# Larger VectorE instructions in the attention, attention weights by offset in DRAM, and four pairs of h scaled when made

## Chip, cores and metric

The kernel runs on 1 core of one Trainium2 chip. The metric is the device time of one execution in microseconds. Engine names: TensorE (PE in the profile, PEld for its weight loads), VectorE (DVE), ScalarE (ACT), GpSimd (POOL), SyncE (SP, which issues DMAs).

## The reference

Sequence 2048, model width 1024, bf16. Two branches and a gate:

```
g = sigmoid((x * gate_w).sum(-1))                        # one number per position
q, k, v = x @ wqkv                                       # 32 heads of 32
logits[h, s, w] = q[h, s] . k[h, s - 2 w] / sqrt(32)     # w = 0..7, masked before the start
a = (sum over w of softmax(logits)[h, s, w] * v[h, s - 2 w]) @ wo
b = (gelu(x @ w_gate) * (x @ w_up)) @ w_down             # hidden width 3584
out = g * a + (1 - g) * b
```

The attention looks at 8 positions per query only, so its products are elementwise work for VectorE and not matmuls.

## The kernel before

The sequence is cut into two halves `s` of 1024 positions. The large products use the Strassen-Winograd scheme: 7 products of quarter size in place of 8, with sums and differences of the operands (the "forms") made by VectorE.

**Units.** The first part of the program is a list of 78 units. Each one makes two 128-row tiles of q and k, of v, or of one pair of the gate or up projection for one half: 7 products of 4 matmuls each, 28 matmuls of 128x512 (L366). A unit overlaps the next: `p1` (L376) of the unit, `p73` (L398) of the unit before, then `p5`, `p26` and `p4` (L406). In `p73` VectorE adds two banks (L403); `p4` writes to one of those banks again, so TensorE waits at `p4` until L403 is done. VectorE takes its instructions in order, so L403 stands behind whatever was put in VectorE's queue earlier.

**Background work.** Between units, `run_bg` (L442) hands out other VectorE work. Each piece is a generator that issues one instruction and yields its planned cost in microseconds; `run_bg` adds 4.7 or 4.8 to `credit` per unit (more where the unit has extra matmuls) and takes pieces by priority while the credit is over 0.3. This is decided when the program is built, so the cost values order the instructions and nothing is decided on the chip. The pieces that matter here:

- `qk_prods` (L610): q times the 8 shifted k of a block of 256 positions, one 128x2048 instruction per block (`qk_mult`, L597, at L598). Three of four blocks of each half are done from the unit's tile; the fourth is `spill` (L639), which multiplies (L598) and adds (L649). TensorE reduces the products over the head with a matrix of ones (L603).
- `softmax`, `softmax_exp` (the exponential, on ScalarE, L697), `softmax_back` (L700): the weights of a block, in `attn_all` as 32 partitions for each quarter `j` of 64 positions. L712 stores them on GpSimd's queue to `w_d`, one DMA for each `j`.
- `pv_all` (L727): per block of 256 positions, `pv_load` (L718) loads the weights (L720) and v (L723) on SP's queue. For each of 8 tiles `t`, L745 multiplies the weights with 8 shifted v (128x2048). `fold` (L752) then adds halves three times (4, 2 and 1 offsets left), two tiles at a time: 128x2048, 128x1024, 128x512. The result goes to `o_d` (L775).
- `t_forms` (L864): four differences of parts of the down weights per group, 128x1024 each (L874), stored to `t_d` (L877). Groups are loaded on SP's queue by `tf_load` (L860).
- `sums_pair` (L318): four forms per pair of gate and up weights (L323).
- `h_task` (L495), which calls `h_store` (L253): gelu(gate) times up, 128x2048 (L254). For pairs 12 and 13 (`i >= NE_`, 12 of 14) the product is multiplied by 1 - g at once (L257). L260 stores it to `h_d`.
- `scale_task` (L913): the h of pairs 0 to 11, loaded again for the down product, is multiplied by 1 - g in place, four pairs per instruction (L918). A11, A12, A21 and A22 are the four blocks of h and attention for one half.

The h of pair 13 of the first half is a special case: its `h_task` may run in the same unit in which its tile is finished, not one later.

```
uu.fin = lambda: bg(h_task(ug.T, uu.T, i, s), *((5.5, now[0]) if (i, s) == (NPAIR - 1, 0) else (7.5 if i == NPAIR - 1 else 0, now[0] + 1)))
```

**Down stage.** `down(0)` and `down(1)` (L1066) multiply the scaled h and the attention with `w_down` and `wo`. `mm` (L1075) is a plain product, `level2` (L1037) a second level of the same scheme with 256-column matmuls (L1046). The forms of its operands are `comb_task` (L927), `forms_L` (L1004) and `forms_R` (L1012); joins are L1031 and outputs L1084, all on VectorE in the order in which they are written.

Of the kernel before, what the change touches and what calls it, by code (L numbers as in the profile page):

```python
# [15 lines left out]
P = 128  # L16
# [52 lines left out]
def kernel(  # L69
# [67 lines left out]
    with tc.manual_schedule(engines={mybir.EngineType.PE, mybir.EngineType.DVE, mybir.EngineType.Activation,  # L137
# [114 lines left out]

        def h_store(G, U, i, s):  # L253
            TT(out=flat(G), in0=flat(G), in1=flat(U), op=ALU.mult)  # L254
# [326 lines left out]
        ab_ = [reg4(R_AB[i], NJ, NWIN, SJ) for i in range(2)]  # L581
        ob_ = [reg3(R_O[i], NT, AC) for i in range(2)]
        prod2 = [reg4(R_PROD2 + 8 * i, 2, NJ, NWIN * SJ) for i in range(2)]

        def mask_init():
            V.memset(mask, 0.0)
# [23 lines left out]
        def qk_prods(u, s, t):  # L610
            while reduced[0] < NT * s + t - t % 2:
                yield None
            out_ = []
            for a in range(ND):
                pr = prod_tile()
                qk_mult(pr, u.T[:, 0, a * AC:(a + 1) * AC], u.T[:, 1, a * AC:(a + 1) * AC])
                out_.append(pr)
                yield 1.14
# [16 lines left out]
        def spill_load(s):  # L635
            nc.sync.dma_start(out=qb[s], in_=q_d[s][:])
            nc.sync.dma_start(out=kb[s], in_=k_d[s][:])

        def spill(s):  # L639
            while reduced[0] < 2 * NT:  # L640
                yield None
            accs = []
            temps = [prod_tile() for _ in range(2)]

            def mult(t, dst):
                qk_mult(dst, qb[s][:, t, :], kb[s][:, t, HALO:HALO + AC])

            def add(g, t):
                TT(out=accs[g], in0=accs[g], in1=temps[t % 2], op=ALU.add)  # L649

            for g in range(NT // QG):
                accs.append(prod_tile())
                mult(QG * g, accs[g])
                yield 1.14
                for t in range(1, QG):
                    mult(QG * g + t, temps[t % 2])
                    yield 1.14
                    if t > 1:
                        add(g, t - 1)
                        yield 1.14  # L660
                add(g, QG - 1)
                yield 1.2
            slotq.append(lambda: spill_reduce(s, accs))

        slotq = []
# [34 lines left out]
        def softmax_back(a, cnt, ee, e4, sw, m, bc):  # L700
            while a // BPS not in gated:
                yield None
            d = m
            V.tensor_reduce(out=d, in_=sw, axis=AX.X, op=ALU.add)
            yield 0.9 * cnt + 0.05
            V.reciprocal(out=d, in_=d)
            TT(out=d, in0=d, in1=gblk[:, a:a + cnt, :], op=ALU.mult)
            yield 0.65 * cnt
            TT(out=attn_all[:, a:a + cnt, :].rearrange("p a (w s) -> p a w s", w=NWIN), in0=e4, in1=bc(d), op=ALU.mult)
            yield 0.55 * cnt + 0.05  # L710
            for j in range(NJ):
                nc.gpsimd.dma_start(out=w_d[a:a + cnt, :, j, :].rearrange("a h n -> h a n"),  # L712
                                    in_=attn_all[32 * j:32 * j + 32, a:a + cnt, :])
            ready.update(range(a, a + cnt))
            if a == 2 * BPS - 1:
                two[0] = True

        def pv_load(a, i):  # L718
            src = w_d[a].rearrange("h j n -> h (j n)")
            nc.sync.dma_start(out=ab_[i % 2].rearrange("p j w s -> p (j w s)"),  # L720
                              in_=AP(src.tensor, src.offset,
                                     [[NJ * SC, 32], [0, 4], [1, NJ * SC]]))
            nc.sync.dma_start(out=vb[i % 2], in_=v_d[:, :, a * AC:a * AC + KV])  # L723
# [3 lines left out]
        def pv_all():  # L727
# [5 lines left out]
            for i, a in enumerate(PVO):  # L733
                if i + 1 < NBLK:
                    while PVO[i + 1] not in ready:
                        yield None
                    pv_load(PVO[i + 1], i + 1)
                if i == 0:
                    pv_task[0].prio = 5
                    tasks.sort(key=lambda t_: t_.prio)  # L740
                    yield None
                v, ab, o_ = vb[i % 2], ab_[i % 2], ob_[i % 2]

                def mult(t):
                    TT(out=prod2[(t // 2) % 2][:, t % 2], in0=ab,  # L745
                       in1=_win_ap(v[:, t, HALO:HALO + AC], [[SJ, NJ], [-DIL, NWIN], [1, SJ]]), op=ALU.mult)

                def fold(t, w):
                    pr = prod2[(t // 2) % 2]
                    h = lambda k: pr[:, :, :, k * w * SJ:(k + 1) * w * SJ]  # L750
                    out_ = h(0) if w > 1 else o_[:, t:t + 2, :].rearrange("p t (j s) -> p t j s", j=NJ)
                    TT(out=out_, in0=h(0), in1=h(1), op=ALU.add)  # L752

                mult(0)
                yield 1.14
                mult(1)
                yield 1.14
                for t in range(0, NT, 2):
                    if i + 1 == NBLK and t == 2:
                        load_A(Bs(0)["A12"], 0, 1, 0, 0, KX, False)  # L760
                    nxt = t + 2 < NT
                    if nxt:
                        mult(t + 2)
                        yield 1.14
                    fold(t, 4)
                    yield 1.14
                    if nxt:
                        mult(t + 3)
                        yield 1.14
                    fold(t, 2)  # L770
                    yield 0.68
                    fold(t, 1)
                    yield 0.4
# [90 lines left out]
        def t_forms():  # L864
            for q in range(NQ):
# [200 lines left out]
        def down(s):  # L1066
# [215 lines left out]
```

## Time and profile before

| | us |
|---|---|
| median of 3 runs (lowest, highest) | 720.89 (720.57, 721.55) |
| span of the profiled execution | 719.0 |
| TensorE matmul busy | 707.4 |
| VectorE busy, 721 instructions | 673.0 |
| ScalarE busy | 328.5 |
| GpSimd busy | 134.1 |
| DMA, mean over the span | 225 GB/s |

The granted TensorE clock is at full speed in all 40 slices but for 0.97 in the last 20 us. The profile is one execution; "idle before" in a row is time in which that engine had nothing running, followed by what ended it. A row "L745 DVE x64 | 77.0, 1220" is 64 instructions of line 745, 77.0 us busy, 1220 ns each. In the timeline the first column is the start in us from the start of the span and the second the duration; equal neighbours are merged, with their number at the end.

### The profile page before, as it was taken

To read this page: it belongs to the slowest core of one execution; us is meant where nothing else is said; L and a number is where in the kernel's file an instruction comes from. 1 tells how busy PE (TensorE), PEld (TensorE's weight loads), DVE (VectorE), ACT (ScalarE), POOL (GpSimd) and SP (SyncE) were. 2 spreads that over 40 slices of the span, in tenths; PEclk is the share of its full clock that TensorE was granted. 3 is DMA by queue.
4 is the path that set the end of the run, shared out by engine and by line. 5 is a ranking of instruction groups with operands and counts; after the bars stand their busy time and mean duration, and the time that the engine had idled before them with its cause. 6 is when DMAs were issued, how large, how long until landed. Compare 5 with 4: busy or idle time off the path is not lost. (4 is left out here: it accounts for less than half of the span.)

```text
span 719.0 us, 10748 instructions
## 1 busy us (share of the span) xinstructions
PE 707.4 (98%) x4051; PEld 408.3 (57%) x4107; DVE 673.0 (94%) x721; ACT 328.5 (46%) x600; POOL 134.1 (19%) x233
## 2 busy tenths in 40 slices
PE   8999999999999999999999999999999999999997
PEld 4466656655544444444444444444447886758886
DVE  2789989999999999999999999999999999899997
ACT  4554546444456665555555555555322321231421
POOL 1323544133210332121200000000210002110011
PEclk9999999999999999999999999999999999999999
DMA  9976743278264758574935746371891799995941
GB/s 276 283 176 227 229 142 133 98 248 303 100 206 128 234 190 254 171 227 142 294 111 155 279 134 210 120 285 59 314 421 60 301 405 399 422 427 217 379 196 60
DMA packets 91748, 162.04 MB, mean 225 GB/s; under 512 B 19264, under 2 KB 68320, under 8 KB 87344
## 3 DMA queue, kind: packets, MB, share of 16 engines
q1 hardware_dynamic: 74992, 105.46, 43.0%
q0 software_dynamic: 15984, 48.29, 19.3%
q10 hardware_dynamic: 720, 7.60, 2.7%
q8 instruction: 32, 0.52, 0.3%
q14 instruction: 20, 0.16, 0.1%
HBM read 112.17 MB, written 54.14 MB: 231 GB/s over the span
## 5 line engine op out<-in xcount | busy, mean ns | idle before, releaser
L366 PE MATMUL banks<-arena 128*128 128x512 bf16 x2136 | 472.1, 379 | 4.2 <-DVE arena L403 0.7
L366 PEld LDWEIGHTS <-arena 128*128 128x128 bf16 x2184 | 240.4, 111 | 235.3 <-issue 7.0
L1046 PE MATMUL banks<-arena 128*128 128x256 bf16 x1260 | 138.7, 273 | 0.6 <-DVE arena L1012 0.6
L1046 PEld LDWEIGHTS <-arena 128*128 128x128 bf16 x1260 | 123.1, 98 | 16.4 <-issue 1.1
L403 DVE TENSOR_TENSOR arena<-banks,arena 128x1024 bf16<-128x1024 f32 x78 | 95.2, 1221 | 11.0 <-PE banks L366 5.4
L389 ACT COPY arena<-banks 128x512 f32<-128x512 f32 x78 | 45.7, 586 | 130.8 <-PE banks L366 130.8
L374 ACT CAST arena<-banks 128x512 bf16<-128x512 f32 x102 | 59.6, 584 | 42.4 <-PE banks L366 42.4
L745 DVE TENSOR_TENSOR arena<-arena 128x2048 bf16<-128x2048 bf16 x64 | 77.0, 1220 | 0.5
L752 DVE TENSOR_TENSOR arena<-arena 128x2048 bf16<-128x2048 bf16 (+2 forms) x96 | 73.9, 776 | 1.0
L598 DVE TENSOR_TENSOR arena<-arena 128x2048 bf16<-128x2048 bf16 x64 | 74.7, 1219 | 0.1
L1075 PE MATMUL banks<-arena 128*128 128x512 bf16 x282 | 62.5, 379 | 0.3
L260 POOL DMA_DIRECT2D h_d<-arena x28 | 20.4, 728 | 226.6 <-DVE arena L254 195.5
L396 ACT COPY banks<-banks 128x512 f32<-128x512 f32 x78 | 44.5, 570 | 21.9 <-PE banks L366 20.1
L1004 DVE TENSOR_TENSOR arena<-arena 128x2304 bf16<-128x2304 bf16 x40 | 53.3, 1352 | 0.5
L384 ACT COPY banks<-banks 128x512 f32<-128x512 f32 x78 | 45.0, 576 | 13.6 <-PE banks L366 12.1
L1051 ACT COPY banks<-banks 128x256 f32<-128x256 f32 x60 | 21.4, 356 | 60.1 <-PE banks L1046 59.9
L1075 PEld LDWEIGHTS <-arena 128*128 128x128 bf16 x288 | 28.2, 98 | 33.6
L927 DVE TENSOR_TENSOR arena<-arena 128x2048 bf16<-128x2048 bf16 (+1 forms) x40 | 41.8, 1112 | 1.6 <-DMA arena<-h_d 1.6
L372 ACT ACTIVATE arena<-banks 128x512 bf16<-128x512 f32 x54 | 32.2, 597 | 15.4 <-PE banks L366 15.4
L323 DVE TENSOR_TENSOR arena<-arena 128x1024 bf16<-128x1024 bf16 x60 | 38.7, 685 | 0.5
L1012 DVE TENSOR_TENSOR arena<-arena 128x2304 bf16<-128x2304 bf16 x28 | 37.7, 1352 | 0.2
L254 DVE TENSOR_TENSOR arena<-arena 128x2048 bf16<-128x2048 bf16 x28 | 34.1, 1216 | 1.9 <-ACT arena L251 1.4
(90 smaller groups left out, 435.4 us busy)
## 6 DMA issues: line engine op xcount, KB each, us to landing
arena<-t_d SPq DMA_DIRECT2D x8, 2304.0 KB, 14.8
h_d<-arena POOLq DMA_DIRECT2D x28, 512.0 KB, 4.3
arena<-w_c SPq DMA_DIRECT2D x12, 1152.0 KB, 13.4
t_d<-arena POOLq DMA_DIRECT2D x36, 256.0 KB, 4.3
arena<-h_d SPq DMA_DIRECT2D x6, 1536.0 KB, 11.8
arena<-in_B_w_gate_dram SPq DMA_DIRECT2D x15, 512.0 KB, 5.7
arena<-in_B_w_up_dram SPq DMA_DIRECT2D x15, 512.0 KB, 4.9
arena<-in_B_w_down_dram SPq DMA_DIRECT2D x28, 256.0 KB, 6.7
```

The source lines that it names most:

```text
L366: self.pe = nc.tensor.matmul(ps, lhsT=self.L[form](kt), rhs=rhs[:, kt, :], start=(start and kt == 0), stop=(kt == HK - 1), skip_group_chec ...
L374: nc.scalar.copy(out=o_, in_=i_)
L384: nc.scalar.copy(out=self.Y, in_=self.X)
L389: nc.scalar.copy(out=self.p5s, in_=self.V)
L396: nc.scalar.copy(out=self.Z, in_=self.Y)
L403: TT(out=self.T[:, :, c2s], in0=pair, in1=self.p5s.rearrange("p (o n) -> p o n", o=1).to_broadcast([P, 2, SC]), op=ALU.add)
L598: TT(out=dst, in0=q.rearrange("p (o s) -> p o s", o=1).to_broadcast([P, NWIN, AC]), in1=_win_ap(k, [[-DIL, NWIN], [1, AC]]), op=ALU.mult)
L745: TT(out=prod2[(t // 2) % 2][:, t % 2], in0=ab, in1=_win_ap(v[:, t, HALO:HALO + AC], [[SJ, NJ], [-DIL, NWIN], [1, SJ]]), op=ALU.mult)
L752: TT(out=out_, in0=h(0), in1=h(1), op=ALU.add)
L1004: TT(out=o_, in0=a, in1=b_, op=op)
L1046: nc.tensor.matmul(c(i, h, j), lhsT=l[:, kt, j * P:(j + 1) * P], rhs=r[:, kt, :], start=False, stop=(kt == KH - 1), skip_group_check=True)
L1075: nc.tensor.matmul(ps, lhsT=L[:, i, j * P:(j + 1) * P], rhs=R[:, i, :], start=(start and q == 0), stop=(q == NK - 1), skip_group_check=not ...
```

## The change

- `qk_prods` and `spill` make two products in one 128x4096 instruction (`qk_mult2`, `pair_at`) where the credit is over 1.5, else one as before. `spill` adds two pairs of sums in one instruction and no longer multiplies into two temporaries in turn. The order of the product tiles in memory changes (`pr_off`, `SPILL`).
- `w_d` holds the weights by offset and position, `[block, head, 8, 256]`. The store is one DMA for each `j` and block, in runs of 64 positions; the load is as large as before. In `pv_all` the shifted v is then read in runs of 256.
- `pv_all` works on four tiles at a time: products of two tiles and first halvings of four tiles in one 128x4096 instruction where the credit is over 1.5, else one tile and two tiles; the second halving is 128x2048, the third 128x1024. Products and halvings are no longer interleaved.
- `t_forms` makes two of its four differences in one instruction.
- h of pairs 8 to 11 is multiplied by 1 - g in `h_store`, and `scale_task` stops at pair 8 (`NSC`). The first half of `down` takes two pieces and not three before its outputs.

```diff
+    NSC = NE_ - 4
-    w_d = tc.dram_tile([NBLK, 32, NJ, SC], BF16, name="w_d")
+    w_d = tc.dram_tile([NBLK, 32, NWIN, AC], BF16, name="w_d")
...
-            if i >= NE_:
+            if i >= NSC:
...
-            yield 1.14 if i < NE_ else 2.35
+            yield 1.14 if i < NSC else 2.3
...
-        pr_off = [R_PR + 4 * i for i in range(4)] + [R_PROD + 4 * i for i in range(2)]
+        pr_off = [R_PR, R_PR + 4, R_PROD, R_PR + 8, R_PR + 12, R_PROD + 4]
...
+        def pair_at(a, b):
+            return _win_ap(reg(a, NWIN * AC), [[int((b - a) * KB), 2], [1, NWIN * AC]])
+
+        def qk_mult2(dst, q, k, sq, sk):
+            TT(out=dst, in0=_win_ap(q, [[sq, 2], [0, NWIN], [1, AC]]),
+               in1=_win_ap(k, [[sk, 2], [-DIL, NWIN], [1, AC]]), op=ALU.mult)
...
+            while a < ND:
+                if a == 0 and credit[0] > 1.5:
+                    qk_mult2(pair_at(pr_off[k], pr_off[k + 1]), u.T[:, 0, 0:AC], u.T[:, 1, 0:AC], AC, AC)
+                    a += 2
+                    yield 2.21
+                else:
+                    qk_mult(out_[a], u.T[:, 0, a * AC:(a + 1) * AC], u.T[:, 1, a * AC:(a + 1) * AC])
+                    a += 1
+                    yield 1.14
...
             for j in range(NJ):
-                nc.gpsimd.dma_start(out=w_d[a:a + cnt, :, j, :].rearrange("a h n -> h a n"),
-                                    in_=attn_all[32 * j:32 * j + 32, a:a + cnt, :])
+                for i in range(a, a + cnt):
+                    nc.gpsimd.dma_start(out=w_d[i][:, :, j * SJ:(j + 1) * SJ],
+                                        in_=attn_all[32 * j:32 * j + 32, i, :].rearrange("h (w s) -> h w s", w=NWIN))
...
+                def mult(t, m):
+                    TT(out=prod2[:, t % 4:t % 4 + m, :],
+                       in0=flat(ab).rearrange("p (o n) -> p o n", o=1).to_broadcast([P, m, NWIN * AC]),
+                       in1=_win_ap(v[:, t, HALO:HALO + AC], [[KV, m], [-DIL, NWIN], [1, AC]]), op=ALU.mult)
+
+                def fold(t, m, w):
+                    h = lambda k: prod2[:, t % 4:t % 4 + m, k * w * AC:(k + 1) * w * AC]
+                    TT(out=h(0) if w > 1 else o_[:, t:t + m, :], in0=h(0), in1=h(1), op=ALU.add)
+
+                for t in range(0, NT, 4):
+                    if i + 1 == NBLK and t == 4:
                         load_A(Bs(0)["A12"], 0, 1, 0, 0, KX, False)
+                    for step, n_ in ((lambda u, m: mult(u, m), 2), (lambda u, m: fold(u, m, 4), 4)):
+                        u = t
+                        while u < t + 4:
+                            m = n_ if u == t + 4 - n_ or n_ == 2 and u % 2 == 0 else n_ // 2
+                            m = m if credit[0] > 1.5 else n_ // 2
+                            step(u, m)
+                            u += m
+                            yield 2.21 if m == n_ else 1.14
+                    fold(t, 4, 2)
                     yield 1.14
+                    fold(t, 4, 1)
+                    yield 0.61
...
-                for o_, a, b_ in ((r11, r12, r11), (r12, r22, r12), (r22, r22, r11), (r21, r21, r22)):
+                n_ = NP * SC
+                both = _win_ap(flat(r11), [[n_, 2], [1, n_]])
+                TT(out=both, in0=_win_ap(flat(r12), [[2 * n_, 2], [1, n_]]), in1=both, op=ALU.subtract)
+                yield 1.14
+                for o_, a, b_ in ((r22, r22, r11), (r21, r21, r22)):
                     TT(out=flat(o_), in0=flat(a), in1=flat(b_), op=ALU.subtract)
-                    yield 0.71
+                    yield 0.61
...
             om = omgrep[:, t0:t0 + SC].rearrange("p (o s) -> p o s", o=1)
+            ib = min(ib, NSC)
...
-                take(rest, 3)
+                take(rest, 2)
```

More of the change, by code (lines that the diff above doesn't have):

```diff
@@ L580 @@
         mask = reg3(R_MASK, NWIN, SJ)
-        ab_ = [reg4(R_AB[i], NJ, NWIN, SJ) for i in range(2)]
+        ab_ = [reg3(R_AB[i], NWIN, AC) for i in range(2)]
         ob_ = [reg3(R_O[i], NT, AC) for i in range(2)]
-        prod2 = [reg4(R_PROD2 + 8 * i, 2, NJ, NWIN * SJ) for i in range(2)]
+        prod2 = reg3(R_PROD2, 4, NWIN * AC)
         def mask_init():
@@ L612, in qk_prods @@
                 yield None
[L613 to L618, printed above, removed]
+            assert ND == 3 and pr_n[0] % 3 == 0
+            k = pr_n[0] % 6
+            out_ = [prod_tile() for _ in range(ND)]
+            a = 0
+            while a < ND:
[7 more added lines that the diff above has]
+                    yield 1.14
             prods[t] = out_
@@ L637, in spill_load @@
             nc.sync.dma_start(out=kb[s], in_=k_d[s][:])
+        SPILL = ((((R_PR, R_PR + 4), (R_PR + 8, R_PR + 12)), ((R_PR + 8, R_PR + 12), (R_PROD, R_PROD + 4))),
+                 (((R_PROD, R_PROD + 4), (R_PR + 4, R_PR + 12)), ((R_PR + 4, R_PR + 12), (R_PR, R_PR + 8))))
         def spill(s):
@@ L642, in spill @@
             accs = []
[L643 to L653, printed above, removed]
-                yield 1.14
[L655 to L662, printed above, removed]
+            for g, (x, y) in enumerate(SPILL[s]):
+                for i, ef in enumerate((x, y)):
+                    t = QG * g + 2 * i
+                    if credit[0] > 1.5:
+                        qk_mult2(pair_at(*ef), qb[s][:, t, :], kb[s][:, t, HALO:HALO + AC], AC, KV)
+                        yield 2.21
+                        continue
+                    for j in range(2):
+                        qk_mult(reg3(ef[j], NWIN, AC), qb[s][:, t + j, :], kb[s][:, t + j, HALO:HALO + AC])
+                        yield 1.14
+                if credit[0] > 1.5:
+                    TT(out=pair_at(*x), in0=pair_at(*x), in1=pair_at(*y), op=ALU.add)
+                    yield 2.21
+                else:
+                    for j in range(2):
+                        TT(out=reg(x[j], NWIN * AC), in0=reg(x[j], NWIN * AC), in1=reg(y[j], NWIN * AC), op=ALU.add)
+                        yield 1.14
+                lo, hi = (reg3(o, NWIN, AC) for o in x)
+                TT(out=lo, in0=lo, in1=hi, op=ALU.add)
+                yield 1.14
+                accs.append(lo)
             slotq.append(lambda: spill_reduce(s, accs))
@@ L718, in pv_load @@
         def pv_load(a, i):
-            src = w_d[a].rearrange("h j n -> h (j n)")
-            nc.sync.dma_start(out=ab_[i % 2].rearrange("p j w s -> p (j w s)"),
+            src = w_d[a].rearrange("h w n -> h (w n)")
+            nc.sync.dma_start(out=flat(ab_[i % 2]),
                               in_=AP(src.tensor, src.offset,
@@ L754, in pv_all @@
[L754 to L759, printed above, removed]
-                        load_A(Bs(0)["A12"], 0, 1, 0, 0, KX, False)
[L761 to L765, printed above, removed]
-                    yield 1.14
[L767 to L773, printed above, removed]
+                def mult(t, m):
+                    TT(out=prod2[:, t % 4:t % 4 + m, :],
+                       in0=flat(ab).rearrange("p (o n) -> p o n", o=1).to_broadcast([P, m, NWIN * AC]),
+                       in1=_win_ap(v[:, t, HALO:HALO + AC], [[KV, m], [-DIL, NWIN], [1, AC]]), op=ALU.mult)
@@ L872, in t_forms @@
                 r11, r12, r21, r22 = tf_set(q)
[L873 removed]
+                n_ = NP * SC
+                both = _win_ap(flat(r11), [[n_, 2], [1, n_]])
+                TT(out=both, in0=_win_ap(flat(r12), [[2 * n_, 2], [1, n_]]), in1=both, op=ALU.subtract)
+                yield 1.14
+                for o_, a, b_ in ((r22, r22, r11), (r21, r21, r22)):
                     TT(out=flat(o_), in0=flat(a), in1=flat(b_), op=ALU.subtract)
[L875 removed]
+                    yield 0.61
                 for k, t in enumerate((r11, r22, r12, r21)):
```

8 lines of the change are left out of this document (removed).

## The prediction

> **What bounds the kernel now.** I began with the page: the busy line of each engine and the slices.
>
> ```profile
> PE 707.4 (98%) x4051; PEld 408.3 (57%) x4107; DVE 673.0 (94%) x721; ACT 328.5 (46%) x600; POOL 134.1 (19%) x233
> PE   8999999999999999999999999999999999999997
> DVE  2789989999999999999999999999999999899997
> ```
>
> TensorE is busy in every slice and VectorE nearly so. TensorE's share is modelled, so I checked it by the starts of single matmuls: outside the first 26 us they follow each other every 0.2158 us (512 columns) or 0.109 us (256 columns), with a few gaps. 0.60 at 43.44 is a weight load's. Those that VectorE or ScalarE causes are 0.47 at 118.85 (ScalarE's exponential and its table load), 0.62 at 175.79, 0.16 at 201 (a table load), 0.13 at 237, 0.45 at 510.20, 0.79 at 663.36 and 0.18 near 682: 2.8 us in all. So TensorE sets the time, and a change on VectorE can win at most about 2.8 us, while it can lose any amount if it makes VectorE late.
>
> Next the timeline of VectorE in the stage of the attention's second half:
>
> ```profile
> 301.98 1.22 DVE L403 TENSOR_TENSOR arena<-banks,arena 128x1024 bf16<-128x1024 f32 x1
> 303.11 1.22 DVE L254 TENSOR_TENSOR arena<-arena 128x2048 bf16<-128x2048 bf16 x1
> 304.24 1.22 DVE L745 TENSOR_TENSOR arena<-arena 128x2048 bf16<-128x2048 bf16 x1
> 305.38 1.22 DVE L752 TENSOR_TENSOR arena<-arena 128x2048 bf16<-128x2048 bf16 x1
> 306.51 1.22 DVE L745 TENSOR_TENSOR arena<-arena 128x2048 bf16<-128x2048 bf16 x1
> 308.00 1.23 DVE L403 TENSOR_TENSOR arena<-banks,arena 128x1024 bf16<-128x1024 f32 x1 [0.26 <-issue]
> ```
>
> Two things: one unit of TensorE (from L403 to L403, 28 matmuls of 0.2158) lasts 6.04 us, and I call it a slot; and a 128x2048 instruction that lasts 1.22 lets the next one start after 1.135, so the queue is to be counted in starts. The same count gives 0.602 for 1024 columns and 0.34 for 512; an instruction that needs the one just before it starts 0.115 later still (1.25 between two that depend, 0.72 at 1024).
>
> Then the two places where TensorE waits for VectorE near the end of the loop and in the second half of the down product:
>
> ```profile
> 505.40 1.22 DVE L254 TENSOR_TENSOR arena<-arena 128x2048 bf16<-128x2048 bf16 x1 [0.48 <-ACT arena L374]
> ...
> 508.93 1.22 DVE L403 TENSOR_TENSOR arena<-banks,arena 128x1024 bf16<-128x1024 f32 x1
> ...
> 510.20 2.75 PE L366 MATMUL banks<-arena 128*128 128x512 bf16 x12 [0.28 <-DVE arena L403]
> ```
>
> ```profile
> 656.68 5.36 DVE L1004 TENSOR_TENSOR arena<-arena 128x2304 bf16<-128x2304 bf16 x4
> ...
> 661.96 2.81 DVE L1012 TENSOR_TENSOR arena<-arena 128x2304 bf16<-128x2304 bf16 x2
> ...
> 663.36 4.87 PE L1046 MATMUL banks<-arena 128*128 128x256 bf16 x43 [0.62 <-DVE arena L1012]
> ```
>
> The first also gives the slack of a slot. L403 frees TensorE 1.27 us after its start (508.93 to 510.20; 174.52 to 175.79 likewise). Undelayed, this L403 would have started at 501.38 + 6.04 = 507.42, and TensorE would have come for it at 510.20 - 0.45 = 509.75, 2.33 later. So L403 may be 2.33 - 1.27 = 1.06 us late for nothing; each us beyond goes to the end.
>
> **The change, part by part.** *Larger instructions.* No row has 4096 columns. The rows are straight: 0.602 at 1024, 1.135 at 2048 (both 0.533 per 1024 and 0.069), 1.268 at 2304. Continued, 4096 costs 2.20, and two merged into one save 0.07. Bounds: 2.13 (no fixed part) and 2.29 (no overlap with the next: 1.22 + 2 x 0.533); I take 2.20, being on the line. The new patterns (three free dimensions, a zero step) are in L745 and L598 already, at full rate. The Trainium skill (Vector Engine (DVE) Microarchitecture Reference, "Measured stream behaviour on trn2") puts about 75 ns per instruction beside the streaming, for sizes up to 8192; that would make 2.21 and leave the sum as it is, and no row here has the size to test it.
>
> Counts are from the built order of the changed program, since a pair is merged only where the credit is over 1.5. Values: products 64 x 1.135 = 72.6 become 20 x 2.20 + 24 x 1.135 = 71.2; the first halving 32 x 1.135 = 36.3 becomes 12 x 2.20 + 8 x 1.135 = 35.5; the second 32 x 0.602 = 19.3 becomes 16 x 1.135 = 18.2; the third 32 x 0.34 = 10.9 becomes 16 x 0.602 = 9.6: -4.6. Logits: 64 x 1.135 become 21 x 2.20 + 22 x 1.135: -1.5. Spilled sums -0.2, weight forms (36 x 0.602 to 9 x 1.135 + 18 x 0.602) -0.6. Together -6.9 us of VectorE, all beside TensorE.
>
> *h of pairs 8 to 11.* Eight more L257 of 1.135 within the loop, +9.1 (and 0.115 each, as L257 needs L254: +0.9); two fewer L918 there, -2.0; seven fewer after the loop, -7.2 in all. So the loop's queue is about as long as before (-6.9 + 9.1 + 0.9 - 2.0 = +1.1 in 470 us) and the down stage's is shorter.
>
> *What reaches TensorE.* Down stage: from 630.08 to 664.69 VectorE runs without a gap, and two of the L918 between are gone (one of A21, one of A22), so L1012 ends 2 x 1.135 = 2.27 earlier. The 0.79 at 663.36 and the 0.18 near 682 go; late next are the matmuls themselves. **-0.97.** In the first half of that stage no matmul waits, so the removed L918 are worth nothing there.
>
> Last slots of the loop: the product with the values ends one slot sooner. The product L254 of pair 13's first half runs in the slot in which its unit ends, and waits for ScalarE's L374 (until 505.36). Before, 2.4 us of L752 stood ahead of that wait; now nothing does, so VectorE idles there from 502.52 and starts L254 at the same 505.40. Behind it stand L257 and now two L918 in place of one (the second comes forward from the next slot), and behind those L403, for which TensorE waits: L403 at 510.07 in place of 508.93, a stall of 0.45 + 1.13. **+1.13.**
>
> Value slots: I carried lateness from slot to slot (queue plus 1.135 less 6.04, never below zero, slack 1.06). The kernel before gives no loss, as its trace shows but for 0.13. The changed one has queues as 2.20 + 2.32 + 1.25 + 1.135 = 6.90 (a merged product, a merged first halving, a second halving and L403 in one slot), and is 1.06 to 1.33 late in ten slots: 0.9 us lost. Six of the ten overshoots are within 0.1, less than the rows settle; ends 0 and 0.9, I take **+0.5.**
>
> Logits and softmax: about as late as before (0.62 and 0.13 before; the six weight forms in slots near 170 are as long). 0, ends -0.3 and +0.3.
>
> *Weights by offset.* The store L712 goes from 20 DMAs (1.7 to 3.1 us to landing) to 32, in pieces of 128 bytes. Nearest row: gblk<-g_d, 128-byte pieces, 16 KB, 5.4 us; with twice the pieces up to 11 us. Cover: blocks 0 and 1 are stored at 148 to 153 and loaded at 234.9, block 7 at 259 and 429. On GpSimd's queue 12 more issues of 0.5 to 0.6 stand ahead of the q, k and v stores, up to 6.6 us in one place; their tiles are written again four or five slots (24 to 30 us) later. Nothing, then; with the cover gone each us comes back through L403. SP: one block's loads move ahead of one weight pair and one behind; the pair's sums come 10 us after its load, which lands in 5.7. The first form of a weight group now needs the fourth load as well; that lands by about 54.3 (47.55 + 6.7) and is needed at 55.1.
>
> **Sum.** -0.97 + 1.13 + 0.5 = +0.7 us. The profiled execution spans 719.0, so 719.7; the median of the runs is 720.89, 1.9 above the span, so 721.6. A measurement of this kernel can tell about 0.2%, 1.4 us, from no change.
>
> **Rivals.** *Slower: 4096 dearer than the line.* At 2.25 the same carry loses 2.4 in the value slots in place of 0.9, at 2.30 3.9: 723.1 to 724.6. It decides from about 2.25. For it: no row of this size, and the queue is at the slack's edge. Against: the straight rows.
>
> *Slower: small pieces.* If stores of 128 bytes took many times as long, stores on GpSimd's queue behind them, and the DMA engines (busy 0.9 of 160 to 180), would hold tiles that L403 writes; two such waits of 2 us past the slack give 723.7. Against: 24 us of cover. The Trainium skill (DMA: Bandwidth & Descriptors, "Specifications") says that pieces under 512 bytes are read, modified and written and miss line rate; by that rule these stores slow down, and no row of the kernel before shows this one.
>
> *Faster: VectorE is late no more.* If pieces fall well (the wait at 505 overlapped, no overshoot), 0.97 + 0.62 + 0.13 + 0.45 = 2.2 goes: 718.7. Against: the built order puts the wait where I say.
>
> *The change does less than it says:* the credit splits 24 of 64 products; already counted.
>
> **Chances.** Forecast 0.56 (720.7 to 722.3 by its terms' ends, all within 0.2%); dearer 4096 0.26; small pieces or another late wait 0.10; faster 0.08. So faster 0.08, same 0.56, slower 0.36. Range 720.0 to 724.0: below it the faster rival, above it the far ends of the slower ones.
>
> **What would show it.** 4096-column starts 2.20 apart; an idle of some 2.9 us before L254's successor near 502.5 and a matmul gap of 1.5 to 1.6 after it; no gap at 663; gaps of 0.1 to 0.3 between 250 and 500. Wrong: starts over 2.25 apart, L403 released by a DMA, or no idle near 502.5.

## Result and profile after

The changed kernel takes 722.14 us (median of 12 runs, 721.35 to 724.36), the kernel before 720.77 in the runs beside it (12 runs, 720.51 to 723.22). The ratio is 1.0019, 95% interval 1.0012 to 1.0026: slower by 0.19%, at the edge of what this measurement can tell. The forecast was 721.6. The profiled execution spans 720.3, before 719.0.

The busy line and VectorE's slices of the page after:

```profile
PE 708.0 (98%) x4051; PEld 408.7 (57%) x4107; DVE 664.3 (92%) x623; ACT 328.6 (46%) x600; POOL 142.0 (20%) x245
DVE  2789979989999999999999999999779998899996
```

VectorE has 98 instructions and 8.7 us less to do, and the kernel gained nothing from it: TensorE is as busy as it was.

The lines have moved in the changed kernel. The lines named up to L550 are one lower in the file: L254 is L255, L403 is L404. Of the logits' products, L598 is L599, and the merged ones are L606; L745 and L752 of the values are L765 and L771. In the down stage L918 is L937, L927 is L946, L1004 and L1012 are L1023 and L1031, L1031 is L1050, L1046 is L1065, and ScalarE's copies L1051 are L1070. The experiments built from it differ by a few lines; scale_only and scale_alone have the lines of the kernel before, one or two lower.

From here on a gap is the time between the starts of two matmuls less 0.2158 (0.109 for 256 columns), and a number in brackets behind it is where it ends. The first gap of the units (0.6 us, near 43 us) comes at another time in every profile (43.20 to 45.50), with the same code ahead of it. So I compare profiles by the time **from that gap to the end**: before 719.0 - 43.44 = 675.6, after 720.26 - 43.60 = 676.7, 1.1 more.

The timeline of VectorE near 171 us of after, with the new size:

```profile
171.43 2.28 DVE L606 TENSOR_TENSOR arena<-arena 128x4096 bf16<-128x4096 bf16 x1
173.63 1.22 DVE L599 TENSOR_TENSOR arena<-arena 128x2048 bf16<-128x2048 bf16 x1
174.76 1.22 DVE L404 TENSOR_TENSOR arena<-banks,arena 128x1024 bf16<-128x1024 f32 x1
```

4096 columns start 2.20 before the next one: the line through the smaller sizes holds.

The timeline at the end of the loop (VectorE, then TensorE, then ScalarE):

```profile
502.05 1.23 DVE L404 TENSOR_TENSOR arena<-banks,arena 128x1024 bf16<-128x1024 f32 x1 [0.77 <-ACT banks L385]
506.07 1.22 DVE L255 TENSOR_TENSOR arena<-arena 128x2048 bf16<-128x2048 bf16 x1 [2.79 <-ACT arena L375]
507.32 1.23 DVE L258 TENSOR_TENSOR arena<-arena,omgrep 128x2048 bf16<-128x2048 bf16 x1
508.47 2.35 DVE L937 TENSOR_TENSOR arena<-arena,omgrep 128x2048 bf16<-128x2048 bf16 x2
510.74 1.22 DVE L404 TENSOR_TENSOR arena<-banks,arena 128x1024 bf16<-128x1024 f32 x1
...
512.01 2.75 PE L367 MATMUL banks<-arena 128*128 128x512 bf16 x12 [1.42 <-DVE arena L404]
...
511.15 0.58 ACT L375 CAST arena<-banks 128x512 bf16<-128x512 f32 x1 [1.66 <-DMA h_d<-arena]
```

VectorE stands idle for 2.79 us ahead of L255, and L258 and two L937 then stand between the wait and L404. TensorE's gap is 1.58 (before 0.45). The last row is one I had not thought of: ScalarE also waits here, for a store of h.

And the down stage, VectorE and TensorE:

```profile
537.41 1.29 DVE L946 TENSOR_TENSOR arena<-arena 128x1024 bf16<-128x1024 bf16 x2 [5.31 <-DMA arena<-h_d]
...
661.75 2.81 DVE L1031 TENSOR_TENSOR arena<-arena 128x2304 bf16<-128x2304 bf16 x2
...
649.80 20.43 PE L1065 MATMUL banks<-arena 128*128 128x256 bf16 x184
```

The gap of 0.79 near 663 is gone, but VectorE waits 5.3 us (before 1.6) for the h of pairs 12 and 13, and works without a pause from there until 580, where a gap of 0.25 appears (582.31).

All gaps that VectorE or ScalarE causes; before: 0.47 (119), 0.62 (176), 0.16 (201), 0.13 (237), 0.45 (510), 0.79 (663), 0.17 (681), together 2.8. After: 0.34 (73), 0.47 (119), 0.36 (176), 0.16 (201), 0.19, 0.10, 0.12 and 0.14 (268, 281, 365, 498), 1.58 (512), 0.25 (582), 0.18 (667), together 3.9. The difference is the 1.1 above.

### The profile page after: what moved, and what is told of

The parts are those of the page before. It is cut to its first block, busy times and chain, and to the rows that moved or that the text cites. A ratio compares the mean times of both kernels' runs of the same rounds, so it can differ in the third digit from the quotient of the medians.

```text
span 720.3 us, 10651 instructions
## 1 busy us (share of the span) xinstructions
PE 708.0 (98%) x4051; PEld 408.7 (57%) x4107; DVE 664.3 (92%) x623; ACT 328.6 (46%) x600; POOL 142.0 (20%) x245
## 4 chain that ended last, share of the span: by engine, by line
PE 58%; DVE 2%; issue 0%; DVEq 0%; ACT 0%
PE banks L367 32%; PE banks L1065 18%; PE banks L1094 9%; DVE arena L1031 0%; DVE arena L1173 0%; DVE arena L937 0%; DVE banks L1050 0%; DVE arena L1023 0%; DVE arena L255 0%; DVE arena L258 0%; DVE arena L404 0%; DVE omgrep L1103 0%; DVEq L1296 0%; DVE arena L1103 0%; ACT arena L375 0%
## 5 line engine op out<-in xcount | busy, mean ns | idle before, releaser
L1065 PE MATMUL banks<-arena 128*128 128x256 bf16 x1260 | 138.7, 273 | 0.1
L1065 PEld LDWEIGHTS <-arena 128*128 128x128 bf16 x1260 | 123.2, 98 | 15.7 <-issue 0.5
L404 DVE TENSOR_TENSOR arena<-banks,arena 128x1024 bf16<-128x1024 f32 x78 | 95.0, 1219 | 12.0 <-PE banks L367 7.8
L375 ACT CAST arena<-banks 128x512 bf16<-128x512 f32 x102 | 59.6, 585 | 44.5 <-PE banks L367 40.4
L765 DVE TENSOR_TENSOR arena<-arena 128x2048 bf16<-128x2048 bf16 (+1 forms) x44 | 73.9, 1705 | 0.4
L771 DVE TENSOR_TENSOR arena<-arena 128x2048 bf16<-128x2048 bf16 (+2 forms) x52 | 67.7, 1303 | 0.8
L1023 DVE TENSOR_TENSOR arena<-arena 128x2304 bf16<-128x2304 bf16 x40 | 53.3, 1352 | 0.5
L1070 ACT COPY banks<-banks 128x256 f32<-128x256 f32 x60 | 21.4, 356 | 59.5 <-PE banks L1065 59.3
L606 DVE TENSOR_TENSOR arena<-arena 128x4096 bf16<-128x4096 bf16 x21 | 47.9, 2283 | 0.3
L946 DVE TENSOR_TENSOR arena<-arena 128x2048 bf16<-128x2048 bf16 (+1 forms) x40 | 41.8, 1112 | 5.3 <-DMA arena<-h_d 5.3
L255 DVE TENSOR_TENSOR arena<-arena 128x2048 bf16<-128x2048 bf16 x28 | 34.1, 1216 | 4.2 <-ACT arena L375 2.8
L1031 DVE TENSOR_TENSOR arena<-arena 128x2304 bf16<-128x2304 bf16 x28 | 37.7, 1352 | 0.2
```

The costliest lines, as they stand in the source:

```text
L375: nc.scalar.copy(out=o_, in_=i_)
L404: TT(out=self.T[:, :, c2s], in0=pair, in1=self.p5s.rearrange("p (o n) -> p o n", o=1).to_broadcast([P, 2, SC]), op=ALU.add)
L606: TT(out=dst, in0=_win_ap(q, [[sq, 2], [0, NWIN], [1, AC]]), in1=_win_ap(k, [[sk, 2], [-DIL, NWIN], [1, AC]]), op=ALU.mult)
L765: TT(out=prod2[:, t % 4:t % 4 + m, :], in0=flat(ab).rearrange("p (o n) -> p o n", o=1).to_broadcast([P, m, NWIN * AC]), in1=_win_ap(v[:, t ...
L771: TT(out=h(0) if w > 1 else o_[:, t:t + m, :], in0=h(0), in1=h(1), op=ALU.add)
L1023: TT(out=o_, in0=a, in1=b_, op=op)
```

## Experiments

All are built from the changed kernel unless said otherwise. Ratios are to the kernel before, on the same chip, with 95% intervals; the third column is the one profile's time from the first gap to the end.

| kernel | ratio | from gap to end |
|---|---|---|
| before | 1 | 675.6 |
| after | 1.0019 (1.0012 to 1.0026) | 676.7 |
| large_only | 1.0052 (1.0039 to 1.0064) | 680.4 |
| scale_alone | 1.0105 (1.0089 to 1.0120) | 684.1 |
| no_merge | 1.0007 (0.9996 to 1.0017) | 676.1 |
| h13_behind | 1.0021 (1.0009 to 1.0033) | 678.1 |
| tiles_order | 1.0008 (0.9999 to 1.0017) | 676.6 |
| tiles_h13_s2 | 0.9999 (0.9988 to 1.0009) | 676.0 |
| tiles_qk | 0.9994 (0.9983 to 1.0004) | 675.1 |
| tiles_qk_h13_s2 | 0.9989 (0.9980 to 0.9997) | 674.6 |
| qk_noscale | 0.9992 (0.9982 to 1.0001) | 675.1 |
| all_u13b | 0.9985 (0.9976 to 0.9994) | 674.5 |

**The two halves alone.** large_only undoes the scaling:

```diff
-    NSC = NE_ - 4
+    NSC = NE_
...
-                take(rest, 2)
+                take(rest, 3)
```

> The larger instructions and the weights by offset without the scaling of pairs 8 to 11 (h_store multiplies from pair 12 on again, scale_task covers pairs 0 to 11, three pieces before the outputs). Theory A (the wait for ScalarE in the slot of pair 13 decides): the values end earlier still, so nothing stands ahead of the wait near 505, and behind it stand L255, L258 and three L937 (1.135, 1.135 and 0.87) before L404: the stall after the wait grows by the third piece, 1.58 + 0.87 = 2.45 us, and the gap near 664 of before (0.6 to 0.8) is back, since seven L937 are back. Span 720.3 + 0.87 + 0.8 = 722.0, the run 723.8. Theory B (the scaling in h_store is what costs, being 9 us more of VectorE in the loop): without it the stall near 512 falls back to 0.45 and the run to 720.8 or lower. Theory C (the value slots' large instructions cost most): about as after, 722.1, with the gaps between 250 and 500 as in after and no more than 1.6 near 512.

The end of the loop in its timeline, and the place of the old gap in the down stage:

```profile
508.97 3.23 DVE L937 TENSOR_TENSOR arena<-arena,omgrep 128x2048 bf16<-128x2048 bf16 x3
512.11 1.22 DVE L404 TENSOR_TENSOR arena<-banks,arena 128x1024 bf16<-128x1024 f32 x1
...
513.38 4.44 PE L367 MATMUL banks<-arena 128*128 128x512 bf16 x12 [2.29 <-DVE arena L404]
...
668.22 4.05 PE L1065 MATMUL banks<-arena 128*128 128x256 bf16 x34 [0.62 <-DVE arena L1031]
```

Three L937 behind the wait, a gap of 2.45 to the digit, and 0.78 at 668: theory A stands, and B falls. Without the scaling the kernel gets slower, so it isn't the scaling that costs. The profile is 1.8 us above the 722.0 expected, and two things more than make that up (the gaps of 0.25 and 0.14 that after has at 582 and 498 are gone). One is a gap of 0.78 at 59.4 (see tiles_order). The other is in the row of 12 matmuls that takes 4.44: after the stall eight of them start 0.427 apart in place of 0.216, 1.7 us more. No expectation had that; it is taken up in the last section. Without these two the time from the first gap is still 1.2 above that of after.

scale_only put the scaling alone into the kernel before:

> The kernel before with the scaling of pairs 8 to 11 in h_store alone (the product of pair 13's first half is put out at the latest before its loads). Theory A: the loop's queue is 9.1 us longer less two L920, nothing pays for it, and the product with the values ends in the last slots; the queue in the last slot is 9.9 us for a slot of 6.04, so TensorE waits about 3.7 us at the last L404 (near 512 to 520), and the stall of 0.45 at 510 is gone; down stage: seven pieces fewer, the gap of 0.79 at 663 gone unless the later h of pair 13 brings a new one. Span 719.0 + 3.7 - 0.45 - 0.97 = 721.3, the run 723.1, more if the late h delays its loads. Theory B (the scaling costs its instructions, and larger ones give nothing): run 722 to 724, but with the lost time spread over slots from 250 on. Theory C (the scaling is free and the down stage gains): run 719.8 to 720.5.

It took 1.0216 (1.0202 to 1.0231). The product with the values did not end before the loads of pairs 12 and 13 were put out: two pairs of A22 were overwritten, so the kernel computes something else, and the last halving waited 10.7 us for a load. Its time is no price of the scaling. The repeat:

> The kernel before with the scaling of pairs 8 to 11 in h_store alone, as scale_only, with the product with the values finished before the loads of pairs 12 and 13 are put out (in scale_only these loads went to memory that the last halvings still used: two pairs of A22 were overwritten, and the last halving waited 10.7 us for a load). Theory A: without larger instructions the loop has no room for 9.1 us more: the last slot's queue is 9.9 us and TensorE waits 3.8 us at the last L404; the loads of A22 and of the rest go out near 513 in place of 505 and may cost as much again. From the first gap to the end 675.6 + 3.8 to 10, ratio 1.004 to 1.014. Theory C (the scaling alone is the gain): 674.6, ratio 0.9985.

VectorE and TensorE at the end of its loop:

```profile
510.50 3.46 DVE L753 TENSOR_TENSOR arena<-arena 128x1024 bf16<-128x1024 bf16 x5
...
518.55 1.22 DVE L404 TENSOR_TENSOR arena<-banks,arena 128x1024 bf16<-128x1024 f32 x1
...
519.82 1.87 PE L367 MATMUL banks<-arena 128*128 128x512 bf16 x4 [3.87 <-DVE arena L404]
```

A gap of 4.0 here, then matmuls at half rate, and 2.5 at 588, behind a wait of 7.3 of VectorE for pairs 12 and 13; the loads went out at 514. As theory A has it, the scaling alone costs 1%, and with the rest of the change 0.2%: what the larger instructions save makes room for it. The 4096 columns are not needed for that, as the next run shows.

**Is it the size?**

```diff
-                if a == 0 and credit[0] > 1.5:
+                if a == 0 and credit[0] > 99:
```

(and so at the other three places of the bound).

> The changed kernel with the credit bound for merged instructions out of reach: no instruction of 4096 columns, all else as in after (four tiles at a time, halvings of 2048 and 1024, weights by offset, scaling in h_store). Theory A: the product with the values ends one slot later, so that one halving of 1024 runs ahead of the wait at 505 and one L937 in place of two behind it: stall near 512 0.45 or less (after 1.58), gap at 663 still gone, value slots with one or two gaps of up to 0.35, up to 1.0 near 150 where the queue of the products is longer. Span 718.5 to 719.5, the run 720.3 to 721.3: 0.8 to 1.8 us less than after. Theory C (size itself costs in the value slots): the gaps between 250 and 500 vanish (0.76 in after), the one at 512 stays 1.58: run 721.4. Theory D (weights in 128-byte pieces and DMAs on GpSimd's queue make it slow): no change from after, 722.1.

```profile
504.91 0.68 DVE L771 TENSOR_TENSOR arena<-arena 128x1024 bf16<-128x1024 bf16 x1
506.75 1.23 DVE L255 TENSOR_TENSOR arena<-arena 128x2048 bf16<-128x2048 bf16 x1 [1.16 <-ACT arena L375]
...
509.15 1.22 DVE L937 TENSOR_TENSOR arena<-arena,omgrep 128x2048 bf16<-128x2048 bf16 x1
```

One halving ahead of the wait, one L937 behind it: the gap is 0.45 (at 511.56). The gaps between 250 and 500 do not vanish: 0.17, 0.25 and 0.13, 0.55 in all, as in after (0.19 + 0.10 + 0.12 + 0.14; the 0.76 of the expectation counted a missing matmul record). So C falls: the value slots cost the same with and without 4096 columns. The logits lose more without it, 1.35 at 176.7 and 0.29 at 148, so the total gains only 0.5. D falls as well: the pieces are the same in this kernel and the gap at 512 is 1.13 smaller, and each gap of after is accounted for by VectorE's L404 or forms, or by ScalarE. In after the 32 stores of w_d, in pieces of 128 bytes, land after 2.1 us (median; before 1.7 for the same 32 KB in longer pieces). The Trainium skill (DMA: Bandwidth & Descriptors, "Specifications") has pieces under 512 bytes miss line rate; the 0.4 us agree in sign. The profile puts one wait of ScalarE's L375 (1.8 us, until 155.3) down to such a store, which the kernel before does not have, but no matmul waits behind it.

**What stands ahead of the wait.**

```diff
-            uu.fin = lambda: bg(h_task(ug.T, uu.T, i, s), *((5.5, now[0]) if (i, s) == (NPAIR - 1, 0) else (7.5 if i == NPAIR - 1 else 0, now[0] + 1)))
+            uu.fin = lambda: bg(h_task(ug.T, uu.T, i, s), *((6.5, now[0]) if (i, s) == (NPAIR - 1, 0) else (7.5 if i == NPAIR - 1 else 0, now[0] + 1)))
```

> The changed kernel with the product of pair 13's first half at priority 6.5 in place of 5.5, so that the two L937 of its slot stand ahead of it and run within the wait for ScalarE. Theory A: L404 starts at 508.5 in place of 510.7 and the gap of 1.58 near 512 vanishes. The product itself starts when it did (about 506.1), its h is stored and loaded when it was, so VectorE's wait of 5.3 us for it near 537 ends when it did; from there VectorE has no idle until 580 and TensorE, now 1.58 us earlier, waits at 582 for 0.25 + 1.58 = 1.8 in place of 0.25. So the gain is given back later: span 720.3 within 0.3, the run 721.9 to 722.3. Rival: VectorE's lateness at 582 has slack or the loads land earlier as TensorE does: span 718.7, the run 720.5.

```profile
505.85 2.35 DVE L937 TENSOR_TENSOR arena<-arena,omgrep 128x2048 bf16<-128x2048 bf16 x2
508.72 1.23 DVE L255 TENSOR_TENSOR arena<-arena 128x2048 bf16<-128x2048 bf16 x1 [0.52 <-ACT arena L375]
...
511.12 1.22 DVE L404 TENSOR_TENSOR arena<-banks,arena 128x1024 bf16<-128x1024 f32 x1
...
515.31 1.02 PE L367 MATMUL banks<-arena 128*128 128x512 bf16 x4 [1.20 <-ACT banks L397]
```

The total is as expected by its ratio, 1.0021 beside 1.0019, and the reason isn't. L404 is in time now, but a few matmuls later ScalarE makes a gap of 1.36, and near 582, where theory A had the time come back, there is none. A second wait stood right behind the first, of about its size. This profile also shows a gap of 1.85 at 61.4, which led to the next kernel.

**Order of the product tiles.** `pr_off` makes R_PROD the third tile; pair 1's gate tile, its h, lies there until it is stored.

```diff
-        pr_off = [R_PR, R_PR + 4, R_PROD, R_PR + 8, R_PR + 12, R_PROD + 4]
+        pr_off = [R_PR, R_PR + 4, R_PR + 8, R_PROD, R_PROD + 4, R_PR + 12]
```

> The changed kernel with another order of the six product tiles, so that R_PROD, where pair 1's gate tile (its h) lies until its store has landed, is the fourth tile and not the third. Theory E (the new tile order makes VectorE wait for that store): the waits of L599 for h_d<-arena near 54 (0.86 in after, 1.64 and 2.71 in two other runs with this order) are gone, and so are the gaps of TensorE that follow: 0.34 at 72.75 in after, 0.78 at 59.4 in large_only, 1.85 at 61.4 in h13_behind. The rest stays (1.58 near 512, 0.25 near 582): span 719.9 in a run without start-up trouble, median 0.3 to 1.0 below after's and a narrower spread than after's 721.35 to 724.36. Rival (the spread comes from the late load of pair 13's h near 537 or from the start of the kernel): median and spread as in after, 722.1.

VectorE's third product, first in h13_behind, then in tiles_order:

```profile
57.36 1.23 DVE L599 TENSOR_TENSOR arena<-arena 128x2048 bf16<-128x2048 bf16 x1 [2.71 <-DMA h_d<-arena]
```

```profile
52.25 2.28 DVE L606 TENSOR_TENSOR arena<-arena 128x4096 bf16<-128x4096 bf16 x1
54.45 1.22 DVE L599 TENSOR_TENSOR arena<-arena 128x2048 bf16<-128x2048 bf16 x1
```

The wait is gone. The gap of 0.34 at 73 is not (0.34 at 72.7), nor is a gap at 59 quite (0.26), so in the profile of after, where the wait was 0.86, it cost nothing; in large_only and h13_behind gaps of 0.8 and 1.9 stand behind it. The median is 0.4 us below after's and the spread as wide (721.04 to 723.36); the two ratios' intervals overlap. That the wait costs something in the median is likely from these profiles and not shown.

**The second wait.** Besides the two moves so far, tiles_h13_s2 puts the four early pieces of the sum S2 ahead of those that need pairs 12 and 13.

```diff
-            run(comb_task(A21, A22, AD, ALU.subtract))
+            run(comb_task(A21, A22, AD, ALU.subtract) if last else comb_task(*C2, LATE))
```

> As tiles_order, with pair 13's product behind the two L937 (as in h13_behind) and with the four early pieces of S2 = A22 - AD put ahead of the pieces that wait for the h of pairs 12 and 13, where VectorE was idle for 3.5 to 5.3 us near 535. Theory A: L404 no longer holds TensorE near 512; what is late next there is ScalarE's L375, whose tile is held by the store of pair 12's h (landed 511.15 in after): 0.2 to 1.4 us are left of the 1.58. VectorE is 4.5 us ahead from 540 to 580, so the gap of 0.25 near 582 is gone and does not grow. Span 720.3 - 0.34 - (0.2 to 1.4) - 0.25 = 718.3 to 719.5, the run 720.1 to 721.3. Rival (given back at 582 all the same, since the late load and not the queue sets that point): a gap of 1 us or more near 582, span 720.

ScalarE's waits of tiles_h13_s2 from 495 to 530 (total, times, longest), and its timeline on TensorE:

```profile
ACT arena L375 <- DMA h_d<-arena: 2.2, 1, 2.2
```

```profile
513.50 1.89 PE L367 MATMUL banks<-arena 128*128 128x512 bf16 x8 [1.39 <-ACT banks L397]
```

The gap is 1.55 (0.2 to 1.4 expected). L375 writes the tile in which pair 12's h (second half) waits for its store. Why that store lands late is in the issues on GpSimd's and SyncE's queue, before and after:

```profile
499.50 0.71 POOL L260 DMA_DIRECT2D h_d<-arena  x1 [11.13 <-ACT arena L372]
...
504.95 0.80 SPq L817 DMA_DIRECT2D arena<-h_d  x2
```

```profile
501.21 0.71 POOL L261 DMA_DIRECT2D h_d<-arena  x1 [11.88 <-ACT arena L412]
...
501.31 0.80 SPq L831 DMA_DIRECT2D arena<-h_d  x2
```

The values end a slot sooner, so the down stage's loads go out 3.6 us earlier (504.95 to 501.31), beside the store and not 5 us behind it. The store's landing shows what that does. Where the loads go out 3.6 us or more behind it (before, no_merge, tiles_qk, tiles_qk_h13_s2) it lands after 3.3 us; where they go out beside it (after, h13_behind, tiles_order, tiles_h13_s2, all_u13 and all_u13b below) after 9.8 to 10.4. In after ScalarE starts at 511.15, ten us after the store's issue. Near 582 nothing is left, and VectorE's wait for pairs 12 and 13 is 0.4 in place of 5.3, as expected.

To take the wait away, the last unit's up half gets another tile. In all_u13 it was pair 12's up tile, in all_u13b 4 KB of pair 12's weights:

```diff
+            if (i, s) == (NPAIR - 1, 1):
+                tu = lambda: reg3(R_RAW[0] + 4, 2, SUP)
```

> As tiles_h13_s2 (all merges kept), and the last unit (up half of pair 13, second half) writes to the tile of pair 12's up half, which is free once L255 has read it, and not to pair 12's gate tile, which is held by the store of its h. Theory F (with L404 in time, the store of pair 12's h, which since the change shares the DMA engines with the loads issued one slot earlier, holds TensorE by way of ScalarE): the wait of L375 for h_d<-arena (2.2 in tiles_h13_s2) and the gap of 1.55 near 513 are gone. From the first gap of the units (43 to 46 us, it differs from run to run) to the end: 676.04 - 1.5 = 674.5, the median 1.5 us below tiles_h13_s2, ratio to before 0.997 to 0.9985. Rival (the wait is for something else, or the next one is as late): a gap of 1 us or more near 513 stays.

It took 1.0165 (1.0151 to 1.0179). There is no gap from 498 to 538, as theory F has it. But the tile that I chose shares memory with T2, one of the forms of the down weights that are loaded from `t_d`. Its load overwrote part of the tile before VectorE read it, so that pair 13's h is changed in this kernel; among VectorE's waits (total, times, longest):

```profile
DVE arena L255 <- DMA arena<-t_d: 18.1, 1, 18.1
```

> As tiles_h13_s2 (all merges kept), with the last unit's up half in 4 KB of pair 12's weights, which are read for the last time four units earlier (in all_u13 its tile shared memory with T2, whose load overwrote part of it and held VectorE 18.1 us). Theory F: no wait of L375 for h_d<-arena, no gap near 513 (1.55 in tiles_h13_s2), and nothing late behind it until the end. From the first gap of the units to the end 676.04 - 1.55 = 674.5 (tiles_qk_h13_s2 674.64), the median near 720.0, ratio to before 0.9975 to 0.9995. Rival (the time comes back at the forms in the down stage): a gap of 0.5 us or more between 580 and 670, 675.5 or more.

```profile
507.75 1.22 DVE L404 TENSOR_TENSOR arena<-banks,arena 128x1024 bf16<-128x1024 f32 x1
...
520.64 13.71 DVE L948 TENSOR_TENSOR arena<-arena 128x2048 bf16<-128x2048 bf16 x12
535.84 1.29 DVE L948 TENSOR_TENSOR arena<-arena 128x1024 bf16<-128x1024 bf16 x2 [1.49 <-DMA arena<-h_d]
...
499.78 12.68 PE L367 MATMUL banks<-arena 128*128 128x512 bf16 x58
```

58 matmuls without a break where after had 1.58, no wait of ScalarE for the store of h (it still lands after 10.4 us, but nobody comes for its tile before that), 1.5 in place of 5.3 of VectorE for pairs 12 and 13 with no gap behind it, and 674.5 from the gap to the end. The median is 719.85 (12 runs, 719.48 to 721.09), faster than before by 0.15% and so, by the two ratios, about 0.34% below after. The whole change is kept here; only its order and two tiles are different.

**The other way round.** Merge only in the logits, so that the values end when they did:

```diff
-                            m = m if credit[0] > 1.5 else n_ // 2
+                            m = n_ // 2
```

> As tiles_order, with merged instructions in the logits only: the product with the values has no 4096-column instruction and ends one slot later, as in no_merge. Theory A: the gap near 511 is 0.45 (no_merge 0.45, after 1.58), the loads of the down stage are issued near 505 in place of 501 and ScalarE's wait for the h store near 511 is 0.5 or less, the gap near 176 is 0.36 (no_merge 1.35) and the one at 148 is gone (no_merge 0.29); in the value slots 0.2 to 0.6 in all. Span 719.4 - 1.0 - 0.3 = 718.1, the run 719.9, ratio to before 0.998 to 0.9995. Rival (value slots' size is what saves VectorE its time, and without it L404 is late there): 1 us or more of gaps between 250 and 500 and no gain over before.

> tiles_qk and the two moves of tiles_h13_s2 together. Theory A: the gap of 0.45 near 511 goes as well, none near 582 or 663: span 717.7, the run 719.5, ratio to before 0.9975 to 0.999. Rival (something late behind takes it back): as tiles_qk.

tiles_qk has 0.36 at 177.6, 0.66 between 250 and 500 and 0.45 at 512.57, near what was expected; its start happened to be late (45.5), and from there it is 1.1 below no_merge (expected 1.3). With the two moves the gap at 512 goes as well. Near 511 ScalarE waits for no store in either; a wait of 1.3 in the first is at 488, for an earlier store, and without a gap behind it.

Last, the scaling taken out of tiles_qk_h13_s2:

> tiles_qk_h13_s2 without the scaling of pairs 8 to 11 in h_store (scale_task covers pairs 0 to 11 again, three pieces before the outputs). What the scaling is worth where the end of the loop does not wait for L404: theory A: in the loop nothing, the L937 of 0.87 that comes forward fits ahead of the wait; the values end one or two slots earlier, so that the loads collide with the store of pair 12's h and up to 1.5 us come at ScalarE near 512; the gap of 0.6 to 0.8 near 665 is back. From the first gap to the end 674.64 + 0.6 to 0.8 + (0 to 1.5) = 675.3 to 676.9, ratio 0.9997 to 1.002. Rival (scaling only moves work): as tiles_qk_h13_s2, 674.6.

675.1: the gap of 0.78 is back (662.9), ScalarE does not wait, and the gaps between 250 and 500 are 0.33 in place of 0.66. The first loads went out from 496.6, ahead of the store; it took 8.8 us to land even so, and was down 0.8 before ScalarE came for the tile. So the scaling is worth its 0.78 in the down stage, less 0.33 in the value slots: about 0.4 us by these two profiles. The medians do not settle it (ratios 0.9992 and 0.9989, with intervals that overlap).

## Why the prediction was right or wrong

- **4096 at 2.20:** right, 2.200 from one start to the next, 2.32 between two that depend. The largest rival (0.26) hung on this and is out.
- **Down stage -0.97:** -0.77. The 0.79 at 663 and the 0.18 near 681 went, as forecast, and 0.18 at 667 is new. The step that failed is "late next are the matmuls themselves": a copy of ScalarE (L1070, 666.37 to 666.74) is, and costs 0.18. Why it starts so late is open; VectorE's join ahead of it comes no later against TensorE than in no_merge, which has no such gap. And in the first half of that stage, where I saw no matmul wait, the wait for pairs 12 and 13 grew by 3.7 us, and VectorE's forms, late by it, brought 0.25 at 582.
- **End of the loop +1.13:** right to the digit and in its mechanism, 1.58. What the step missed is that ScalarE was nearly as late, so that the 1.13 could not have been won back by order on VectorE alone (h13_behind). I had followed the DMAs that are issued later, and not the one whose store collides with loads that are now issued earlier.
- **Value slots +0.5:** 0.55, in four gaps of 0.1 to 0.2 where the working had ten slots and 0.9. The reason given, the merged sizes, is not needed for it: no_merge has 0.55 with none of them, in three other slots. The slots are full either way, in part by the scaling (0.66 with it in tiles_qk_h13_s2, 0.33 without it in qk_noscale). So the size is partly luck.
- **Logits and softmax 0:** right in sum, by luck: +0.34 at 73, -0.26 at 176 and -0.13 at 237 cancel, and none of the three was forecast.
- **Weights by offset 0:** right for TensorE. The cover was not as wide as I had it: ScalarE waited 1.8 us at 155, see no_merge. The 723.7 of the rival with small pieces is the span of 719.7 with two waits of 2 us added; as a median, like the other figures, that is 725.6, outside the range.
- **Not in it:** the order of the product tiles, which I had read as a renaming; it puts a wait of 0.9 to 2.7 us at 54.
- **Sum:** +0.7 forecast; +1.1 by the gaps (0.25 at 582 and 0.20 of the down stage make up the difference), +1.3 in the span with 0.16 of start-up.

## What to carry to other kernels

Work taken off an engine that isn't the bound is not only a gain that may be hidden: it lets what follows start sooner, and here that brought a bare wait at the head of a queue and loads beside a store that someone was waiting for. So after counting a queue, look at what now stands ahead of each wait and which transfers move, and fill the wait with work that needs nothing from it. When one wait is removed and the time stays, look for the next one within its length.

## What the runs showed of the hardware

Behind the longer stalls of TensorE the matmuls ran at half rate for about 3.4 us. In large_only (2.29 idle) eight starts are 0.427 apart, from 514.24 to 517.65, and the granted clock is 0.78 from 512 to 516 and 0.80 from 516 to 520. In scale_alone the rate is halved behind both stalls (3.87 and 2.33 idle; 256 columns 0.213 apart in place of 0.109), and the granted clock is 0.50 from 521 to 523 and from 589 to 591. After 1.42 idle in after and 1.7 in h13_behind (the gap at 61.4) all starts are 0.216 apart. So in these profiles a stall cost its length up to some point between, and 1.7 us more beyond it: the 1.58 of after was not far from costing twice as much.

It need not come in every execution. 3.4 us at half clock make the mean granted clock of large_only 0.998; of its six runs three have 0.999, as runs of the kernel before beside them do, and three 0.996 to 0.998. Where the stall falls may decide. In each profile that has such a stretch (large_only, scale_alone, scale_only, all_u13) the changes of the granted clock lie whole multiples of 3.413 us apart, in scale_alone at 519.84, 523.25, 588.11 and 591.52. Cut into stretches of that length, the clock halves at the end of one in which TensorE idled for 2.29 us or more, and doesn't behind the 1.69 of h13_behind. A stall across the end of a stretch would then be cheaper than the same stall inside one. No run here moves one stall against the stretches, so that is not shown.

The Trainium skill (TensorE: Matmul & The Clock Gate, "Why this matters for your kernels") warns of gaps over about 3 us; here 2.3 was enough. The half clock and the idle window of about 3.4 us that the Trainium skill gives (TensorE: Matmul & The Clock Gate, "What's actually happening") agree with the 0.50 and the 3.4 us.
